# A list planner whose ranks for DVE, ACT and POOL are counted back from TensorE's list, with costs fitted to the trace

## The chip, the cores and the metric

The kernel runs on one core of one Trainium2 chip. The metric is the device time of one execution in microseconds (us), the median of several runs. Engines are named as in the profile: PE is TensorE (its matmuls; PEld its weight loads), DVE is VectorE, ACT is ScalarE, POOL is GpSimd, SP is SyncE.

## The reference

Three stages follow each other over 6016 tokens of width 256, all in float32:

```python
s = kn.transpose(0, 2, 1) @ qn / tau      # 256 x 256 scores of normalised k and q
a = softmax(s)
x = v @ a                                  # 6016 x 256
h = x @ w_in                               # 256 -> 2048
y = (h * sigmoid(1.702 * h)) @ w_out       # 2048 -> 256
gate, val = sigmoid(y @ w_gate), y @ w_val # 256 -> 1536
out = (gate * val) @ w_out2                # 1536 -> 256
```

## The kernel before

The softmax matrix is multiplied into `w_in` first (`m_unit`), so that the first stage is one product of `v` with a 256 x 2048 matrix `m_t`. Each float32 factor is split in two float16 parts, a high part (`gh`, ACT or DVE) and a rest (`gl`, DVE, L314 or L1589), and a product is three matmuls. Tokens come in 12 blocks of 512 (the last has 384). The first two blocks use plain products (`eight`); later ones use Strassen's seven products per 2 x 2 block (`seven`, `gv_pair`, `o_pair`), with additions on DVE and copies on ACT between them. In the first stage a block has 8 units: `h_unit` makes the products into PSUM banks, applies the gelu on ACT (L1181, L1187) and splits the result; `y_unit` multiplies it by `w_out` (L1013 to L1015). In the second stage a block has 6 pairs: `gv_pair` (L1472) with copies (L1480) and sigmoids (L1500) on ACT and adds (L1493), a product (L1524), differences (L1563, L1566, L1569) and splits (L1551, L1589) on DVE, and `o_pair` (L1640). POOL takes some differences and the seven final additions `comb` of each block (L1695). Weights are unpacked (L502, L508, L514), scaled by a power of two and split while the first stage runs: for `w_out` ("o1") that is a chain of small DVE steps ending with `own_wo` (L271), a matmul that spreads it over the partitions (L287), a maximum (L290), two small steps (L299), and the split on ACT and DVE (L311, L314) into `wo`.

All of it is written down first as a list of operations in `Plan`, with engine, cost, and dependencies; `Plan.run` then plays a list schedule with these costs and emits the instructions of each engine in the order found. Each engine runs its own list in order and waits on semaphores. At each step `run` takes the operation that can start first; among those on that engine which can start within a small window (`EPS`, `HOLD`), the one with the lowest rank is preferred. Before, an operation's rank is its place in the program plus a hand-set `delay`:

```python
self.ops.append((fn, engines, deps, i + self.delay, lone))
rank = lambda i: self.ops[i][3]
_, s, e, c, i = min(cand, key=lambda x: (x[1], rank(x[4])))
```

Of the kernel before, what the change touches and what calls it, by code (L numbers as in the profile page):

```python
# [46 lines left out]
class Plan:  # L47
# [53 lines left out]

    def run(self):
        n = len(self.ops)
        after = [[] for _ in range(n)]
# [28 lines left out]
        while ready:  # L133
# [12 lines left out]
            rank = lambda i: self.ops[i][3]  # L146
# [21 lines left out]
def fused_kernel(ctx, tc, q, k, vt, tau, w_in, w_o1, w_g, w_v, w_o2, outt):  # L168
# [180 lines left out]
    def right_ops(z, n, q4, rest, kx, s, ks, after=()):  # L349
# [125 lines left out]
    def w_top(name, i, after=()):  # L475

        wide = w_src[name][1]
        if name in LOOSE:
# [5 lines left out]
            w_op(name, total, ("act", 1.25), r=[("w", name, i)],  # L484
# [10 lines left out]
    def w_f32(name, i, after=()):  # L495
# [30 lines left out]
        w_op(name, mag, ("act", 1.1), r=[kr], w=[kw], after=list(after) + [w_open[name]])  # L526
        w_op(name, shift3, ("dve", 0.68), r=[kw], w=[kw])
        if name in LOOSE:
            w_top(name, i)
        if name in BY_POOL:  # L530
            plan.delay += JOIN * (name == "in")
            w_op(name, sign, ("act", 1.1), r=[kr], w=[kr])
            w_op(name, lambda e: join(0, ALU.logical_shift_right, 29), ("dve", 1.22), r=[kr, kw], w=[kw])
            w_op(name, signed, ("pool", 2.4), r=[kr, kw], w=[kw])
            plan.delay -= JOIN * (name == "in")
        else:
            w_op(name, lambda e: join(1, ALU.bitwise_and, 0x80000000), ("dve", 1.22), r=[kr, kw], w=[kw])
# [42 lines left out]
    def w_split(name, h, lo, i, after=()):  # L580
# [9 lines left out]
        w_op(name, hi, ("act", 1.1), r=r, w=[("wh", name, i)], after=after)  # L590
        w_op(name, low, ("dve", 1.26), r=r + [("wh", name, i)], w=[("wl", name, i)])
# [250 lines left out]
    def softmax(i):  # L842
# [179 lines left out]
    def seven(z, w, left, rl, val):  # L1022
# [8 lines left out]
        def product(a, x, key, start):  # L1031
            def fn(e):
# [8 lines left out]
                op(fn, ("pe", 3 * (w / 2400 + 0.004)), r=rl(a) + [("Th", z, right), ("Tl", z, right)], w=[key])  # L1041
            )

        def copy(dst, key, wk):
            after = a21_users if wk[0] != "rot" and wk not in plan.writer else ()
            op(lambda e: nc.scalar.copy(out=dst, in_=bank(key)[:, :w]), ("act", 0.1 + w / 1150), r=[key], w=[wk],  # L1046
               after=after)

        def add(half, other, ko):
# [729 lines left out]
```

## Time and profile before

| | us |
|---|---|
| median of 3 runs | 1028.23 (1027.2 to 1029.16) |
| the profiled execution's own time | 1027.24 |
| its span, first to last instruction | 1025.2 |
| PE busy | 1016.8 |
| DVE busy | 875.7 |
| ACT busy | 736.6 |
| POOL busy | 122.2 |

In the profile a matmul's end is modelled, so that successive matmuls overlap in the rows; when PE was really held up is read from the distance of two starts, not from a gap. DVE and ACT rows overlap their successor too, by some 0.08 and 0.10 us. A wait is named with what released it.

### The profile page before, as it was taken

The numbers are of one execution on the slowest core, as the hardware profiler recorded it, in microseconds if no ns is written. First come the engines' busy times: TensorE is split into PE (matmuls) and PEld (weight loads), VectorE is DVE, ScalarE is ACT, GpSimd is POOL, SyncE is SP. The second block draws the span as 40 slices with busy tenths as digits, with TensorE's granted clock in tenths as the row PEclk, the third lists the DMA queues.
The fourth block names the chain that finished last, engine by engine and source line by source line (L and its number), as shares of the span: only waits on it lengthen the run. The fifth ranks groups of instructions, "written<-read, shape, count | busy, mean of one in ns | idle before, by whom it ended". The sixth has DMA issues, their size and how long they took to land.

```text
span 1025.2 us, 18922 instructions
## 1 busy us (share of the span) xinstructions
PE 1016.8 (99%) x7709; PEld 767.9 (75%) x7709; DVE 875.7 (85%) x1377; ACT 736.6 (72%) x1193; POOL 122.2 (12%) x145
## 2 busy tenths in 40 slices
PE   9999999999999999999999999999999999999998
PEld 7744456666666666666677788888888888888896
DVE  6999989999888767767598998989889889898984
ACT  6789368877776656556566777787787777787774
POOL 0120100100000000000000002021230330222302
PEclk9999999999999999999999999999999999999999
DMA  9930213210000000000000000000000000000001
GB/s 346 404 121 21 83 42 144 103 62 22 21 1 22 21 1 17 1 1 1 1 2 2 1 22 22 2 21 7 17 22 2 22 21 1 22 7 17 21 3 36
DMA packets 17399, 43.68 MB, mean 43 GB/s; under 512 B 1824, under 2 KB 8224, under 8 KB 15648
## 3 DMA queue, kind: packets, MB, share of 16 engines
q1 hardware_dynamic: 16736, 41.56, 11.3%
q8 instruction: 60, 0.98, 0.4%
q10 hardware_dynamic: 576, 0.92, 0.3%
q14 instruction: 27, 0.22, 0.1%
HBM read 36.31 MB, written 6.16 MB: 41 GB/s over the span
## 4 chain that ended last, share of the span: by engine, by line
PE 91%; DVE 3%; DMA 2%; issue 2%; ACT 1%; POOL 0%; SPq 0%; ACTq 0%; POOLq 0%
PE ps L1472 31%; PE ps L1037 17%; PE ps L1640 13%; PE ps L1015 10%; PE ps L1014 10%; PE ps L1013 10%; PE ps L948 1%; DMA tau<-in_tau 1%; DVE gl L314 1%; DMA m_t<-in_q 1%; DMA m_t<-in_k 1%; DVE vo L314 0%; POOL full_in L524 0%; DVE gf L1051 0%; DVE s_t L314 0%
## 5 line engine op out<-in xcount | busy, mean ns | idle before, releaser
L1472 PE MATMUL ps<-vo,s_t 128*128 128x256 f16 (+1 forms) x3024 | 362.0, 270 | 0.2 <-ACT m_t L1500 0.2
L1472 PEld LDWEIGHTS <-s_t 128*128 128x128 f16 x3024 | 292.6, 98 | 38.2 <-issue 0.6
L1037 PE MATMUL ps<-vo,m_t 128*128 128x256 f16 (+1 forms) x1680 | 217.8, 270 | 0.0
L1037 PEld LDWEIGHTS <-m_t 128*128 128x128 f16 x1680 | 162.6, 98 | 67.9 <-issue 1.0
L1014 PE MATMUL ps<-gl,wo 128*128 128x512 f16 (+1 forms) x348 | 130.2, 374 | 0.0
L1015 PE MATMUL ps<-gh,wo 128*128 128x512 f16 (+1 forms) x348 | 130.2, 374 | 0.0
L1013 PE MATMUL ps<-gh,wo 128*128 128x512 f16 (+1 forms) x348 | 130.2, 374 | 0.0
L1493 DVE TENSOR_TENSOR gf<-ps,m_t 128x512 f32<-128x512 f32 (+1 forms) x144 | 97.3, 676 | 37.2 <-PE ps L1472 31.8
L1500 ACT ACTIVATE m_t<-ps,sgb 128x512 f32<-128x512 f32 (+1 forms) x144 | 97.5, 680 | 41.4 <-PE ps L1472 40.5
L314 DVE SCALAR_TENSOR_TENSOR gl<-gf,sgi,gh 128x1024 f16<-128x1024 f32 (+1 forms) x87 | 109.1, 1255 | 4.2 <-ACT gh L311 3.6
L1046 ACT COPY m_t<-ps 128x256 f32<-128x256 f32 (+1 forms) x160 | 57.5, 364 | 74.4 <-PE ps L1037 73.2
L1480 ACT COPY m_t<-ps 128x512 f32<-128x512 f32 (+1 forms) x144 | 83.0, 576 | 38.7 <-PE ps L1472 34.7
L1051 DVE TENSOR_TENSOR gf<-ps,m_t 128x256 f32<-128x256 f32 (+1 forms) x160 | 65.3, 414 | 42.6 <-ACT m_t L1046 25.6
L1524 DVE SCALAR_TENSOR_TENSOR gf<-gf,m_t 128x1024 f32<-128x1024 f32 (+1 forms) x72 | 88.2, 1229 | 1.9
L1589 DVE TENSOR_TENSOR gl<-ts,gh 128x1024 f16<-128x1024 f32 x60 | 74.4, 1241 | 3.4 <-ACT gh L1586 3.3
L1640 PEld LDWEIGHTS <-wo 128*128 128x128 f16 x720 | 70.3, 98 | 8.0
L1640 PE MATMUL ps<-gh,wo 128*128 128x256 f16 x360 | 76.1, 273 | 0.0
L1695 POOL TENSOR_TENSOR m_t<-m_t 128x256 f32<-128x256 f32 x70 | 65.5, 949 | 67.3 <-ACT m_t L1687 65.1
L1015 PEld LDWEIGHTS <-wo 128*128 128x128 f16 x384 | 37.6, 98 | 43.6
L1204 DVE TENSOR_SCALAR gh<-gf,sgi 128x1024 f16<-128x1024 f32 (+1 forms) x63 | 46.4, 736 | 26.8 <-PE ps L1015 24.6
L1586 ACT CAST gh<-ts 128x1024 f16<-128x1024 f32 x60 | 62.7, 1046 | 6.1 <-DVE ts L1569 3.6
L1181 ACT ACTIVATE gf<-gf,sgs 128x512 f32<-128x512 f32 (+1 forms) x80 | 56.0, 709 | 11.5 <-DVE gf L1051 10.6
(249 smaller groups left out, 1607.1 us busy)
## 6 DMA issues: line engine op xcount, KB each, us to landing
v_raw<-in_vt SPq DMA_DIRECT2D x11, 512.0 KB, 5.0
out_t<-m_t SPq DMA_DIRECT2D x40, 128.0 KB, 1.7
m_t<-in_k SPq DMA_DIRECT2D x9, 512.0 KB, 7.7
m_t<-in_q SPq DMA_DIRECT2D x9, 512.0 KB, 8.6
s_t<-in_w_o SPq DMA_DIRECT2D x3, 1024.0 KB, 4.9
s_t<-in_w_g SPq DMA_DIRECT2D x3, 1024.0 KB, 5.1
s_t<-in_w_v SPq DMA_DIRECT2D x3, 1024.0 KB, 5.0
big<-in_w_in SPq DMA_DIRECT2D x2, 1024.0 KB, 10.5
```

Source lines behind the costliest of these rows:

```text
L314: nc.vector.scalar_tensor_tensor(out=lo, in0=x, scalar=s, in1=h, op0=ALU.mult, op1=ALU.subtract)
L1013: nc.tensor.matmul(ps[:, :n], w_h, x_h, start=first, stop=False)
L1014: nc.tensor.matmul(ps[:, :n], w_h, x_l, start=False, stop=False)
L1015: nc.tensor.matmul(ps[:, :n], w_l, x_h, start=False, stop=last)
L1037: nc.tensor.matmul(dst, l, r, start=start and y == 0, stop=y == 2, skip_group_check=True)
L1472: nc.tensor.matmul(dst, l, r, start=start and f == 0 and y == 0, stop=y == 2, skip_group_check=True)
L1480: op(lambda e: nc.scalar.copy(out=dst, in_=bank(key)[:, : 2 * w]), ("act", 0.12 + 2 * w / 1180), r=[key], w=[wk], after=late_after if wk[0 ...
L1493: nc.vector.tensor_add(quarters(T[kf], half), pairs(bank(kw)), pairs(other))
L1500: nc.scalar.activation(out=quarters(sig_t[ks[1] % 2], half), in_=pairs(bank(key)), func=AF.Sigmoid, scale=T[sk])
L1524: nc.vector.scalar_tensor_tensor(out=v, in0=v, scalar=VSHIFT, in1=sig_t[ks[1] % 2][:, : 4 * w], op0=ALU.mult, op1=ALU.mult)
L1589: nc.vector.tensor_sub(T[name][1][:, : 4 * w], T[kt][:, : 4 * w], T[name][0][:, : 4 * w])
L1640: nc.tensor.matmul(dst, l, r, start=start and p == 0 and y == 0, stop=p == NP2 - 1 and y == 2, skip_group_check=True)
```

## The change

Operations from `plan.first` on (from the first unit of the first stage) get new ranks. The PE operations are laid end to end in the order of their old ranks, which gives each a planned start; from there each DVE, ACT and POOL operation gets a due time, its user's due time less its own cost and 0.17; its rank becomes that of the PE operation planned at that time, and lower still where the due time is negative. The second part is the costs: those of nearly all DVE and ACT operations and of the PE products are set to new values, mostly lower by some per cent. No operation is added or removed; the order in which each engine does them changes, and for operations that two engines can do, the engine.

```diff
+SLACK, EASE = 0.0, 0.0
...
+    def due(self, first):
+
+        ranks = [o[3] for o in self.ops]
+        pe = sorted((i for i in range(first, len(self.ops)) if self.ops[i][1][0][0] == "pe"), key=lambda i: ranks[i])
+        t, at, due = 0.0, [], {}
+        for i in pe:
+            due[i] = t
+            at.append(t)
+            t += self.ops[i][1][0][1]
+        for j in range(len(self.ops) - 1, first - 1, -1):
+            d = due.setdefault(j, t)
+            for i, kind in self.ops[j][2].items():
+                if i >= first and self.ops[i][1][0][0] != "pe":
+                    gap = 0.0 if kind in ("place", "order") else self.LAT + self.ops[i][1][0][1]
+                    due[i] = min(due.get(i, t), d - gap)
+        for i in range(first, len(self.ops)):
+            if self.ops[i][1][0][0] != "pe":
+                x = bisect(at, due[i] + SLACK) - 1
+                ranks[i] = ranks[pe[max(x, 0)]] + min(due[i] + SLACK, 0.0) * 6 + EASE * (due[i] + SLACK - at[max(x, 0)])
+        return ranks
...
-            rank = lambda i: self.ops[i][3]
+            rank = ranks.__getitem__
...
-                op(fn, ("pe", 3 * (w / 2400 + 0.004)), r=rl(a) + [("Th", z, right), ("Tl", z, right)], w=[key])
+                op(fn, ("pe", 3 * (w / 2400 + 0.0023)), r=rl(a) + [("Th", z, right), ("Tl", z, right)], w=[key])
...
-            op(lambda e: nc.scalar.copy(out=dst, in_=bank(key)[:, :w]), ("act", 0.1 + w / 1150), r=[key], w=[wk],
+            op(lambda e: nc.scalar.copy(out=dst, in_=bank(key)[:, :w]), ("act", 0.06 + w / 1200), r=[key], w=[wk],
...
-        op(hi, [("act", 0.14 + 0.93 * f), ("dve", 0.1 + 0.53 * f, GH_DVE)], r=r, w=[k_g],
+        op(hi, [("act", 0.19 + 0.854 * f), ("dve", 0.13 + 0.534 * f, GH_DVE)], r=r, w=[k_g],
```

Over the whole program 25 of the high-part conversions of the first stage (L1204 on DVE, L311 on ACT) move from DVE to ACT and 8 the other way. Of the quarter differences of the second stage (L1566, L1569) 28 move from DVE to POOL and 16 the other way. SP's list is the same but for two neighbouring loads that trade places.

**First place, DVE where the scale of `w_out` is found.** Before, from `own_wo` (the last step ahead of the matmul L287) to the split of `wo`; `mf` and `ms` are sums of `m_t` that the third block's products need, `s_t` and `gl` are rests of units:

```order
L271 TENSOR_SCALAR own_wo_111<-cl_wo_110 128x1
L984 TENSOR_TENSOR mf_858<-m_t 128x1024
L290 TENSOR_REDUCE p_wo_112<-ps 128x1
L989 TENSOR_TENSOR ms_869<-mf_858 128x256
L299 RECIPROCAL s_wo_113<-p_wo_112 128x1
L989 TENSOR_TENSOR ms_869<-mf_858 128x256
L299 TENSOR_SCALAR s_wo_113<-s_wo_113 128x1
L989 TENSOR_TENSOR ms_869<-ms_869,mf_858 128x256
L989 TENSOR_TENSOR ms_869<-mf_858,ms_869 128x256
L314 SCALAR_TENSOR_TENSOR s_t<-y_f,sgi_647,s_t 128x1024
L314 SCALAR_TENSOR_TENSOR wo_87<-big,s_wo_113,wo_87 128x1024 x4
```

And after the change, on the same engine from the same instruction (L295 is now what L271 was, L338 what L314 was):

```order
L295 TENSOR_SCALAR own_wo_111<-cl_wo_110 128x1
L338 SCALAR_TENSOR_TENSOR gl_0_0_690<-gf_0_0_682,sgi_666,gh_0_0_689 128x1024
L314 TENSOR_REDUCE p_wo_112<-ps 128x1
L323 RECIPROCAL s_wo_113<-p_wo_112 128x1
L323 TENSOR_SCALAR s_wo_113<-s_wo_113 128x1
L323 RECIPROCAL s_v_117<-p_v_116 128x1
L338 SCALAR_TENSOR_TENSOR gl_0_1_730<-gf_0_1_720,sgi_666,gh_0_1_729 128x1024
L338 SCALAR_TENSOR_TENSOR wo_87<-big,s_wo_113,wo_87 128x1024 x4
```

The two rests `gl` of the first units, which stood far ahead of `own_wo` before, now stand behind it, and the sums have gone behind the split. In PE's list the matmul L287 on `own_wo` stands 7 products (of `eight`) earlier than before, and the first product of `y_unit` (L1013 on `gh`) follows it after 3 products, where there were 4.

**Second place, ACT in the eighth block of the first stage.** `gf_7_3` is the gelu of unit 3 (in two halves), COPY is a bank that PE will write again; before:

```order
L311 ACTIVATE vo<-tt,s_v_201 128x1024
L1245 COPY big<-ps 128x512 x2
L1181 ACTIVATE gf_7_3_3491<-ps,sgs_3194 128x512
L1046 COPY ps<-ps 128x256 x2
L1046 COPY m_t<-ps 128x256 x2
L1181 ACTIVATE gf_7_3_3491<-gf_7_3_3491,sgs_3194 128x512
```

And after the change, around the same gelu:

```order
L1205 ACTIVATE gf_7_3_3466<-ps,sgs_3025 128x512
L335 ACTIVATE gh_7_1_3479<-gf_7_1_3363,sgi_3026 128x1024
L1205 ACTIVATE gf_7_3_3466<-gf_7_3_3466,sgs_3025 128x512
L335 ACTIVATE vo<-tt,s_v_201 128x1024
L1269 COPY big<-ps 128x512
L1070 COPY ps<-ps 128x256
L1269 COPY big<-ps 128x512
L1070 COPY ps<-ps 128x256
L1070 COPY m_t<-ps 128x256 x3
```

A conversion `gh_7_1` that DVE did before now stands here between the two gelu halves, and the copies of the next units come behind the long operations in one row.

**Third place, DVE at the end of the ninth block of the second stage.** `gf_8_5` belongs to that block's last pair, `gf_9_0` to the next block's first; each pair has two adds from PSUM, and the second frees the bank that the next pair's product L1472 writes. Before, from one second add to the next:

```order
L1493 TENSOR_TENSOR gf_8_5_9823<-ps,m_t 128x2x256
L1524 SCALAR_TENSOR_TENSOR gf_8_5_9823<-gf_8_5_9823,m_t 128x1024
L1493 TENSOR_TENSOR gf_9_0_9882<-ps,m_t 128x2x256
L1589 TENSOR_TENSOR gl_8_4_9874<-ts_8_4_9832,gh_8_4_9873 128x1024
L1563 TENSOR_TENSOR ts_8_5_9906<-gf_8_5_9823 128x512
L1551 TENSOR_TENSOR m_t<-gf_8_5_9823,m_t 128x768
L1566 TENSOR_TENSOR ts_8_5_9906<-gf_8_5_9823,ts_8_5_9906 128x256
L1493 TENSOR_TENSOR gf_9_0_9882<-ps,m_t 128x2x256
```

And after the change, up to the same add of `gf_9_0` (the last row; the second add of `gf_8_5` stands two rows ahead of the first row shown, with one split `vo` of 128x768, L338, between):

```order
L1549 SCALAR_TENSOR_TENSOR gf_8_5_9772<-gf_8_5_9772,m_t 128x1024
L1576 TENSOR_TENSOR m_t<-gf_8_4_9685,m_t 128x768
L1614 TENSOR_TENSOR gl_8_4_9798<-ts_8_4_9748,gh_8_4_9797 128x1024
L1588 TENSOR_TENSOR ts_8_5_9848<-gf_8_5_9772 128x512
L338 SCALAR_TENSOR_TENSOR vo<-tt,s_y_235,vo 128x1024
L1518 TENSOR_TENSOR gf_9_0_9871<-ps,m_t 128x2x256
L1479 TENSOR_TENSOR sgb_9884<-qb_234,kg 128x1
L1594 TENSOR_TENSOR ts_8_5_9848<-gf_8_5_9772,ts_8_5_9848 128x256
L384 TENSOR_TENSOR tt<-big 128x384
L387 TENSOR_TENSOR tt<-big,tt 128x192
L1576 TENSOR_TENSOR m_t<-gf_8_5_9772,m_t 128x768
L1518 TENSOR_TENSOR gf_9_0_9871<-ps,m_t 128x2x256
```

The preparation of a later block's input (`tt`, `vo`, L338, L384, L387), which stood elsewhere before, has come in between. From the second add of `gf_8_4` to the second add of `gf_9_0` DVE's list has 15 instructions before and 24 after the change; PE's list has, between the product that the first of these adds reads and the one that writes the bank again after the second, 35 products (16 of `gv_pair`, of 6 matmuls each, and 19 of `o_pair`, of 3) after the change.

## Rows read from the trace of the kernel before

**Rows 1.** The page, busy time by engine, and granted PE clock in 40 slices.

```profile
PE 1016.8 (99%) x7709; PEld 767.9 (75%) x7709; DVE 875.7 (85%) x1377; ACT 736.6 (72%) x1193; POOL 122.2 (12%) x145
...
PEclk9999999999999999999999999999999999999999
```

**Rows 2.** Busy time by stretch: PE, PEld, DVE, ACT, POOL, clock, DMA, GB/s.

```profile
75.00:150.00 75.00, 75.00 (x372) 36.17 (x371) 68.72 (x104) 48.63 (x57) 3.57 (x3) 1.00 0.15 50
150.00:325.00 175.00, 174.96 (x1174) 114.73 (x1173) 162.93 (x295) 133.72 (x248) 7.97 (x12) 1.00 0.15 53
325.00:525.00 200.00, 200.00 (x1405) 134.62 (x1404) 139.40 (x261) 121.97 (x245) 6.09 (x9) 1.00 0.03 8
...
600.00:1000.00 400.00, 399.99 (x3701) 359.59 (x3700) 363.39 (x488) 307.05 (x466) 83.47 (x97) 1.00 0.04 13
```

**Rows 3.** PE's own waits: us in total, times, longest.

```profile
PE ps L877 <- ACT ex L857: 1.3, 2, 1.0
...
PE ps L1472 <- ACT m_t L1500: 0.2, 1, 0.2
```

**Rows 4.** PE in order of time where a start came late: start, length, instruction.

```profile
254.94 0.38 PE L1015 MATMUL ps<-gh,wo 128*128 128x512 f16 x1
255.32 0.49 PE L1037 MATMUL ps<-vo,m_t 128*128 128x256 f16 x3
...
531.88 0.82 PE L1472 MATMUL ps<-vo,s_t 128*128 128x256 f16 x6
532.93 0.82 PE L1472 MATMUL ps<-vo,s_t 128*128 128x256 f16 x6 [0.24 <-ACT m_t L1500]
...
962.82 0.27 PE L1640 MATMUL ps<-gh,wo 128*128 128x256 f16 x1
963.10 1.14 PE L1472 MATMUL ps<-vo,s_t 128*128 128x256 f16 x9
```

**Rows 5.** ACT in order of time, the table load at 531.

```profile
530.90 1.28 ACT L1500 ACT_TABLE_LOAD   x1
```

**Rows 6.** PE in order of time, the start of the first stage.

```profile
82.25 0.38 PE L1013 MATMUL ps<-vo,m_t 128*128 128x512 f16 x1
...
91.31 0.22 PE L287 MATMUL ps<-ident_b,own_wo 128*128 128x128 bf16 x1
...
96.55 0.38 PE L1013 MATMUL ps<-gh,wo 128*128 128x512 f16 x1
```

**Rows 7.** DVE in order of time, the same stretch.

```profile
68.68 0.75 DVE L1204 TENSOR_SCALAR gh<-gf,sgi 128x1024 f16<-128x1024 f32 x1
...
69.80 0.75 DVE L314 SCALAR_TENSOR_TENSOR m_t<-ps,rss,m_t 128x512 f16<-128x512 f32 x1 [0.36 <-ACT m_t L311]
...
80.81 1.29 DVE L314 SCALAR_TENSOR_TENSOR vo<-v_raw,s_v,vo 128x1024 f16<-128x1024 f32 x1 [0.32 <-ACT vo L311]
...
89.51 0.15 DVE L271 TENSOR_SCALAR own_wo<-cl_wo 128x1 uint32<-128x1 uint32 x1
...
91.57 0.29 DVE L290 TENSOR_REDUCE p_wo<-ps 128x1 f32<-128x128 f32 x1 [0.78 <-PE ps L287]
...
94.88 1.28 DVE L314 SCALAR_TENSOR_TENSOR wo<-big,s_wo,wo 128x1024 f16<-128x1024 f32 x1 [0.24 <-ACT wo L311]
```

**Rows 8.** ACT in order of time, the same stretch.

```profile
93.72 4.25 ACT L311 ACTIVATE wo<-big,s_wo 128x1024 f16<-128x1024 f32 x4
```

**Rows 9.** Groups by line and shape: busy, mean ns of one | idle before.

```profile
L311 ACT ACTIVATE gh<-gf,sgi 128x1024 f16<-128x1024 f32 x23 | 26.4, 1148 | 5.2 <-PE ps L1015 5.0
```

**Rows 10.** DVE in order of time, from `gf_8_4` to `gf_9_0`.

```profile
898.37 0.69 DVE L1493 TENSOR_TENSOR gf<-ps,m_t 128x512 f32<-128x512 f32 x1
...
908.78 0.68 DVE L1493 TENSOR_TENSOR gf<-ps,m_t 128x512 f32<-128x512 f32 x1
```

**Rows 11.** POOL and DVE in order of time, where both run.

```profile
919.35 7.98 POOL L1695 TENSOR_TENSOR m_t<-m_t 128x256 f32<-128x256 f32 x7 [3.73 <-ACT m_t L1687]
...
921.97 1.75 DVE L314 SCALAR_TENSOR_TENSOR vo<-tt,s_y,vo 128x1024 f16<-128x1024 f32 x1
```

More of the change, by code (lines that the diff above doesn't have):

```diff
@@ L1 @@
+from bisect import bisect
 from contextlib import ExitStack
@@ L100, in op @@
         return i
+    def due(self, first):
[17 more added lines that the diff above has]
+        return ranks
     def run(self):
         n = len(self.ops)
+        ranks = self.due(self.first)
         after = [[] for _ in range(n)]
@@ L377, in right_ops @@
         for fn, m in ((t13, 2), (t2, 1), (t4, 1)):
-            op(fn, ("dve", 0.12 + m * w / 930), r=kx, w=[k], after=after)
+            op(fn, ("dve", 0.08 + m * w / 960), r=kx, w=[k], after=after)
         split(3, 4, lambda: tt[:, : 4 * w], [k])
@@ L482, in total @@
                 )
[L484 removed]
+            w_op(name, total, ("act", 1.05), r=[("w", name, i)],
                  w=[("ws", name, i)], after=after)
@@ L524, in signed @@
             nc.gpsimd.tensor_mul(x, x, half(name, i, 1).bitcast(F32))
-        w_op(name, mag, ("act", 1.1), r=[kr], w=[kw], after=list(after) + [w_open[name]])
-        w_op(name, shift3, ("dve", 0.68), r=[kw], w=[kw])
+        w_op(name, mag, ("act", 1.0), r=[kr], w=[kw], after=list(after) + [w_open[name]])
+        w_op(name, shift3, ("dve", 0.61), r=[kw], w=[kw])
         if name in LOOSE:
@@ L589, in w_split @@
         r = [("w", name, i), ("wsc", name)]
-        w_op(name, hi, ("act", 1.1), r=r, w=[("wh", name, i)], after=after)
-        w_op(name, low, ("dve", 1.26), r=r + [("wh", name, i)], w=[("wl", name, i)])
+        w_op(name, hi, ("act", 1.0), r=r, w=[("wh", name, i)], after=after)
+        w_op(name, low, ("dve", 1.2), r=r + [("wh", name, i)], w=[("wl", name, i)])
     def s_ratio(after=()):
@@ L1001, in m_sums @@
         for n_, (out, x, y, how) in enumerate(chain):
-            op(lambda e, out=out, x=x, y=y, how=how: sums(e, out, x, y, how), ("dve", 0.4),
+            op(lambda e, out=out, x=x, y=y, how=how: sums(e, out, x, y, how), ("dve", 0.35),
                r=[kf] + ([ks] if n_ else []), w=[ks] if n_ == 0 else [("ms", fg)])
@@ L1347, in fused_kernel @@
     m_units(M_FIRST)
+    plan.first = len(plan.ops)
     steps = [(b, u) for b in range(NBLK) for u in range(NU)]
@@ L1422, in o2_sums @@
         r = [(k, "o2", i) for k in ("wh", "wl") for i in range(ch * 4 * w // PW, -(-(ch + 1) * 4 * w // PW))]
-        op(blocks4, ("dve", 1.2), r=r, w=[kf], after=after)
+        op(blocks4, ("dve", 1.14), r=r, w=[kf], after=after)
         add, sub = nc.vector.tensor_add, nc.vector.tensor_sub
@@ L1439, in dst @@
             return so[:, y, :, 2 * ch : 2 * ch + 2, :]
-        op(lambda e: nc.scalar.copy(out=dst(0), in_=src()), ("act", 1.1), r=[ks, ("os", ch)], w=[("soh", ch)], after=after)
+        op(lambda e: nc.scalar.copy(out=dst(0), in_=src()), ("act", 1.0), r=[ks, ("os", ch)], w=[("soh", ch)], after=after)
         op(lambda e: nc.vector.tensor_sub(dst(1), src(), dst(0)), ("dve", 1.2), r=[ks, ("os", ch), ("soh", ch)],
@@ L1475, in product @@
             i = 2 * p * P // NB
-            first_op.append(op(fn, ("pe", 6 * (w / 2400 + 0.004)),
+            first_op.append(op(fn, ("pe", 6 * (w / 2400 + 0.0023)),
                                r=[("Sh", i, a), ("Sl", i, a), ("Th", z, right), ("Tl", z, right)], w=[key]))
         def copy(dst, key, wk):
-            op(lambda e: nc.scalar.copy(out=dst, in_=bank(key)[:, : 2 * w]), ("act", 0.12 + 2 * w / 1180), r=[key], w=[wk],
+            op(lambda e: nc.scalar.copy(out=dst, in_=bank(key)[:, : 2 * w]), ("act", 0.06 + w / 600), r=[key], w=[wk],
                after=late_after if wk[0] != "rot" else ())
```

62 lines of the change are left out of this document (31 added, 31 removed).

## The prediction

> **What bounds the kernel now.** The page comes first: PE is busy 1016.8 of 1025.2 us, the granted clock is full in all 40 slices, and DVE (875.7) and ACT (736.6) have slack [rows 1]. The reader is to see that a change which leaves PE's work alone can win only what PE loses by waiting. [...] From 600 to 1000 us 3701 matmuls take 400.0 us, 0.108 us each, so a matmul there follows the one before without pause.
>
> The chain of waits names few for PE [rows 3]: 1.3 us on L857's exponentials are in the softmax ahead of the first unit, where DMA and the scores set the pace, and only one is behind 75 us. Because a PE row's end is modelled, I look instead at the distance of starts. After 60 us only eight starts are more than 0.04 us late, 1.24 us together. Three of them stand in the rows [rows 4]: L1037 at 255.32 comes 0.38 after a matmul of 512 columns, for which 0.21 is the rule in that list (0.17 late); at 963.10 a matmul comes 0.28 after one that needs 0.11 (0.17); and the largest, 0.41, ends at 532.93. In front of this last one ACT loads a table, 1.28 us from 530.90 [rows 5], because the gelu gives way to the sigmoid. Both lists hold the same table loads, so I leave that wait where it is. The other seven make 0.83 us. That is what better ranks can win back in the body of the program, and it is less than a tenth of a per cent.
>
> What lies ahead of 60 us is bound by loads and by the softmax, and the last products and stores of the final block keep their order; the lists first differ on ACT at about 45 us, on DVE at about 62 and on PE at 82.
>
> **The change part by part.** PE does the same products with the same number of columns. The new ranks and the new costs answer one question together, the order, so they are priced together; none costs or saves engine time by itself except by the engine that takes an operation. 17 net conversions go from DVE to ACT: 1.15 us each there [rows 9] for 0.75 on DVE [rows 7], so ACT gains about 19.6 us of work and DVE loses 12.8; 12 net differences leave DVE for POOL. From 150 to 525 us ACT is busy 255.7 of 375 us [rows 2], so both fit on average. The question is only whether a PE operand comes later than its turn at a place where nothing is in reserve.
>
> *Waits of before.* Seven waits, 0.83 us. A new order moves all neighbours, so these can go altogether; I take −0.8, with bounds 0 and −1.2 (the last if the table wait goes too).
>
> *The scale of `w_out`.* This is the place where PE's own order moves. L287 stands 7 products earlier. A product is three matmuls of 512 columns whose starts are 0.43 us apart here, 1.295 us for the three, so PE comes to L287 at 91.31 − 9.06 = 82.25 us and to the first product of `y_unit` at 82.25 + 3 × 1.295 + 0.05, about 86.2 [rows 6]. DVE must have `own_wo` by then. Before, it takes 20.83 us from L1204 at 68.68 to `own_wo` at 89.51 [rows 7]. In the new order there drop out of this stretch four rests `gl` or `s_t` and one split `vo` (rows of this shape are 1.28 long, 1.20 from start to start), one `gh` (0.67 a step), about 0.45 of small steps, and the two idles of 0.36 and 0.32 behind ACT [rows 7]: 6.0 + 0.67 + 0.45 + 0.68 = 7.8. That leaves 13.0; I add 0.5 because ACT does an unpacking ahead of a high part that DVE waits for. So `own_wo` is ready at about 68.68 + 13.5 = 82.2, just as PE arrives. From there the chain goes on: a `gl` (1.20) now stands ahead of the maximum L290 (0.29 [rows 7]), then two small steps of 0.19, the high part on ACT (1.06 a step [rows 8], about 1.13 to its end), the rest on DVE (1.28 [rows 7]): 4.3 us. Against 3.9 on PE's side, the product waits about 0.3 us. What is late next: eight products queued behind it on PE, and a gelu behind the four conversions of `wo` (4.25 us together [rows 8]), about 0.2. Term +0.5; bounds 0.2 and 1.2, the last if `own_wo` is 0.7 us later than worked out.
>
> *Copies behind conversions on ACT.* In the second place ACT now has a conversion between the two halves of a gelu, and a row of copies behind. The adds on DVE that need these copies free PE's banks. Before, with 33 conversions on ACT, six of the seven waits lie between 150 and 525 us and come to 0.65 us, 0.02 for each conversion; without the one at 313 us, behind a maximum of `v` (0.20), it is 0.014. At these prices 50 conversions cost between 0.7 and 1.0 us; I take +0.8, since costs near the true step leave an operation no more reserve than before. It would stand mostly where DVE's adds near 363, 402 and 441 us free a bank. Bounds: 0, because PE may have other work in its queue at each place, and 2.0, 0.04 for each of the 50.
>
> *The end of the ninth block of the second stage.* From second add to second add DVE takes 908.78 − 898.37 = 10.41 us for 15 instructions, 0.69 a step [rows 10]. 24 instructions at that step are 16.7 us. PE has 35 products in between, 16 × 6 + 19 × 3 = 153 matmuls, 16.5 us at 0.108. The margin is gone: any delay there is one of PE's. Term +0.3, bounds 0 (the small rows among the 24 are shorter than the mean) and 0.9 (two collisions with POOL, next).
>
> *Differences on POOL.* While POOL runs its seven additions from 919.35, a rest on DVE takes 1.75 us [rows 11] where the same shape takes 1.28 elsewhere [rows 7], 0.47 more. For 12 more POOL operations that is up to 12 × 0.47 = 5.6 us of DVE, against its 36.6 us idle between 600 and 1000 us [rows 2]; its price for PE is nil except where a margin is nil, and that is in the range of the term before. [...]
>
> **Sum.** −0.8 + 0.5 + 0.8 + 0.3 = +0.8 us. The profiled execution took 1027.24, so 1028.0 on its scale. The runs' median is 1028.23, 1.0 above that execution, so the forecast is **1029.0 us**: a little more PE waiting, in other places than before. A difference of 0.2%, 2.06 us, is about what a measurement of this kernel can tell from none.
>
> **The rivals.** *The waits go.* The ranks are counted back from PE's own list, and if each operand comes in time all of 0.8 to 1.2 us go: 1027.0 to 1027.4 against the median. For it speaks that the average load leaves room on every engine; against it that a rank only prefers among operations that could start nearly at once, and that DVE keeps 90% busy from 600 to 1000 us. The case that the new order changes nothing visible (1028.2) belongs here too.
>
> *`own_wo` late (slower).* If DVE does one maximum of `v` (1.2) and one `gl` (1.2) more ahead of `own_wo` than I count, L287 stands at the head of PE's queue for 2.4 us and everything behind it with it: 1029.0 + 2.4 = 1031.4. It decides for "slower" from 1.3 us of lateness on. For it: the margin is nil by my sum. Against: an item in the list is counted, not guessed; only waits on ACT and loads could shift it.
>
> *DVE blocked by POOL (slower).* Eight collisions more at places without margin, 8 × 0.47 = 3.8, give 1032.8; from four on it is slower by the bound. For it: the cost per collision is in the rows. Against: there are few places without margin, and DVE idles behind PE in most of the second stage.
>
> **How the numbers follow.** The likeliest case, waits that change places, has 0.73, mostly 1028.0 to 1030.2; the waits that go, or nothing visible, 0.10; `own_wo` late 0.08; DVE blocked 0.06; a gain above the 1.2 us that the trace has on offer, from the softmax or the end, 0.03. The range 1026.9 to 1031.5 leaves out the top of the last rivals and the gain beyond 1.3 us. A gain over 0.2% is 0.03; slower than 0.2%, above 1030.3, takes the two slow rivals and a few hundredths of the first case, 0.17; within, 0.80.
>
> **What would show it.** Right: in the rows of PE's start distances a late start of a few tenths at L287 or at the first L1013 on `gh` near 86 us; late L1037 behind DVE adds between 300 and 525 us; a late L1472 near 910 us; those at 255, 271 and 313 us gone; the one behind the table load still there; L1204's count on DVE down by 17, the differences L1566 and L1569 on POOL up by 12, PE's count unchanged. Wrong: PE late by over 1 us at L287, or DVE's rests of 1.75 us beside POOL in many places with late L1472 behind them; or no late start after 60 us at all, by which the ranks would have done what my margins deny.

## The result and the profile after

The changed kernel takes 1036.59 us (median of 5, 1035.98 to 1037.01) against 1027.2 us of the kernel before beside it: ratio 1.0086, 95% interval 1.0071 to 1.0101. It is slower, by more than the forecast range allowed. The profiled execution is one of 1036.59 us with a span of 1034.5, 9.3 us more than before.

First the page and the windows by stretch of the changed kernel, to be read beside [rows 1] and [rows 2] (columns as there):

```profile
PE 1022.1 (99%) x7709; PEld 769.5 (74%) x7709; DVE 872.9 (84%) x1348; ACT 752.9 (73%) x1210; POOL 149.9 (14%) x157
```

```profile
525.00:575.00 50.00, 50.00 (x394) 38.31 (x393) 43.37 (x66) 36.08 (x54) 0.00 (x0) 1.00 0.01 1
575.00:596.00 21.00, 20.46 (x152) 14.66 (x150) 18.67 (x30) 14.85 (x23) 3.01 (x3) 1.00 0.01 5
596.00:604.00 8.00, 4.77 (x42) 4.10 (x42) 4.43 (x8) 2.32 (x5) 0.71 (x1) 1.00 0.15 57
604.00:608.00 4.00, 3.40 (x17) 2.34 (x17) 2.19 (x4) 1.14 (x4) 0.00 (x0) 0.58 0.00 0
608.00:625.00 17.00, 17.00 (x157) 15.24 (x156) 15.06 (x20) 13.97 (x20) 2.96 (x2) 1.00 0.01 1
```

Most of what was lost, 6.35 of 9.0 us, lies in one place, 595 to 608 us: PE idles 3.2 us of eight, and in the four behind it the granted clock is 0.58. PE's own waits, as in [rows 3], name two that were not there before:

```profile
PE ps L1497 <- ACT m_t L1505: 3.4, 1, 3.4
...
PE ps L1497 <- DVE gf L1518: 1.0, 1, 1.0
```

And PE in order of time, as in [rows 4]:

```profile
600.92 0.27 PE L1665 MATMUL ps<-gh,wo 128*128 128x256 f16 x1
604.60 1.44 PE L1497 MATMUL ps<-vo,s_t 128*128 128x256 f16 x6 [3.40 <-ACT m_t L1505]
605.83 0.42 PE L1665 MATMUL ps<-gh,wo 128*128 128x256 f16 x1
```

Six matmuls from 604.60 to 605.83 are about 0.21 us each, where 0.108 is usual, and the granted clock is 0.50 from 604.60 to 607.00 us; 15 starts in a row are like that. So the late starts of this place come to 1.13 (at 596.42) + 3.57 (at 604.60) + 1.65 (the 15 at half clock and the one ahead of them) = 6.35 us. All starts more than 0.04 us late behind 60 us make 10.26, before 1.24; the difference, 9.0, is the span's 9.3 but for some tenths in the prologue. The other 3.9 us are 32 late starts of 0.05 to 0.41 us.

The chain of waits blames ACT's copy L1505 and DVE's add, but both had been done in time if their own engines had not waited. Going back from them in the changed kernel, one engine after the other, first ACT and DVE, then POOL in order of time:

```profile
602.44 1.04 ACT L1611 CAST gh<-ts 128x1024 f16<-128x1024 f32 x1 [3.88 <-POOL ts L1594]
...
603.97 0.58 ACT L1505 COPY m_t<-ps 128x512 f32<-128x512 f32 x1
```

```profile
589.23 0.15 DVE L295 TENSOR_SCALAR own_y<-cl_y 128x1 uint32<-128x1 uint32 x1
...
594.55 0.16 DVE L323 RECIPROCAL s_y<-p_y 128x1 f32<-128x1 f32 x1 [1.96 <-POOL p_y L302]
...
597.01 0.43 DVE L1591 TENSOR_TENSOR ts<-gf,ts 128x256 f32<-128x256 f32 x1
```

```profile
581.15 1.31 POOL L1591 TENSOR_TENSOR ts<-gf,ts 128x256 f32<-128x256 f32 x1 [64.13 <-DVE ts L1588]
586.87 1.32 POOL L1594 TENSOR_TENSOR ts<-gf,ts 128x256 f32<-128x256 f32 x1 [4.40 <-DVE ts L1591]
594.14 0.38 POOL L302 PARTITION_ALL_REDUCE p_y<-own_y  x1 [5.96 <-issue]
601.69 0.71 POOL L1594 TENSOR_TENSOR ts<-gf,ts 128x256 f32<-128x256 f32 x1 [7.17 <-issue]
```

The reader is to see two idles of POOL that nothing in the profile ends ("issue"). The all-reduce of `p_y` (the maximum of the last block of `y` over the partitions) has its input at 589.38 and starts at 594.14; the difference behind it has its input at 597.44 and starts at 601.69. DVE stands 1.96 us behind the first, ACT 3.88 us behind the second, each with its other work queued up, and PE behind both. In the kernel before the same all-reduce ran 40.7 us earlier, and 28.6 us ahead of the first difference:

```profile
553.46 0.35 POOL L278 PARTITION_ALL_REDUCE p_y<-own_y  x1 [37.37 <-DVE own_y L271]
582.45 0.73 POOL L1569 TENSOR_TENSOR ts<-gf,ts 128x256 f32<-128x256 f32 x1 [28.64 <-DVE ts L1566]
```

POOL's list says what is between. Of the kernel before, from the last all-reduce but one, and of the changed one, from the same place (a row with ISA and no operand stands wherever the kind of operation changes; in the built program it is an instruction to reload a library, `PseudoReloadLibraryIndex`, index 1 ahead of all-reduces and 0 ahead of differences; it has no row in the profile):

```
L278 ISA p2_y0_233<-own_y0_232 128x1
L278 ISA p2_y1_238<-own_y1_237 128x1
L1569 ISA
L1569 TENSOR_TENSOR ts2_1_0_5847<-gf2_1_0_5779,ts2_1_0_5847 128x256
```

```
L302 ISA p2_y0_233<-own_y0_232 128x1
L1591 ISA
L1591 TENSOR_TENSOR ts2_1_0_5828<-gf2_1_0_5757,ts2_1_0_5828 128x256
L1594 TENSOR_TENSOR ts2_1_1_5877<-gf2_1_1_5823,ts2_1_1_5877 128x256
L302 ISA
L302 ISA p2_y1_238<-own_y1_237 128x1
L1594 ISA
L1594 TENSOR_TENSOR ts2_1_2_5989<-gf2_1_2_5906,ts2_1_2_5989 128x256
```

Behind its unpacking of weights, POOL's list of before goes over once to the all-reduces (ahead of 73.38 us) and once from them to the differences, both at leisure; the changed one then goes back and over again.

### The profile page after: what moved, and what is told of

The parts are those of the page before. It is cut to its first block, busy times and chain, and to the rows that moved or that the text cites. A ratio compares the mean times of both kernels' runs of the same rounds, so it can differ in the third digit from the quotient of the medians.

```text
span 1034.5 us, 18983 instructions
## 1 busy us (share of the span) xinstructions
PE 1022.1 (99%) x7709; PEld 769.5 (74%) x7709; DVE 872.9 (84%) x1348; ACT 752.9 (73%) x1210; POOL 149.9 (14%) x157
## 4 chain that ended last, share of the span: by engine, by line
PE 90%; issue 3%; DVE 3%; DMA 2%; ACT 2%; POOL 0%; SPq 0%; DVEq 0%; POOLq 0%; ACTq 0%
PE ps L1497 31%; PE ps L1061 17%; PE ps L1665 13%; PE ps L1037 9%; PE ps L1039 9%; PE ps L1038 9%; PE ps L972 1%; DMA big<-in_w_in 1%; DVE big L538 1%; DMA m_t<-in_q 1%; ACT wo L335 0%; DMA m_t<-in_k 0%; ACT sq L748 0%; ACT junk L504 0%; POOL full_in L548 0%
## 5 line engine op out<-in xcount | busy, mean ns | idle before, releaser
L1497 PE MATMUL ps<-vo,s_t 128*128 128x256 f16 (+1 forms) x3024 | 370.4, 271 | 4.5 <-ACT m_t L1505 3.4
L1061 PE MATMUL ps<-vo,m_t 128*128 128x256 f16 (+1 forms) x1680 | 222.3, 270 | 0.0
L1518 DVE TENSOR_TENSOR gf<-ps,m_t 128x512 f32<-128x512 f32 (+1 forms) x144 | 97.4, 677 | 28.6 <-PE ps L1497 16.3
L338 DVE SCALAR_TENSOR_TENSOR gl<-gf,sgi,gh 128x1024 f16<-128x1024 f32 (+1 forms) x87 | 109.0, 1253 | 3.0 <-ACT gh L335 2.7
L1505 ACT COPY m_t<-ps 128x512 f32<-128x512 f32 (+1 forms) x144 | 83.1, 577 | 35.5 <-PE ps L1497 34.1
L1549 DVE SCALAR_TENSOR_TENSOR gf<-gf,m_t 128x1024 f32<-128x1024 f32 (+1 forms) x72 | 92.5, 1285 | 3.4
L1720 POOL TENSOR_TENSOR m_t<-m_t 128x256 f32<-128x256 f32 x70 | 70.2, 1014 | 119.2 <-ACT m_t L1712 117.4
L1614 DVE TENSOR_TENSOR gl<-ts,gh 128x1024 f16<-128x1024 f32 x60 | 75.3, 1255 | 7.7 <-ACT gh L1611 7.4
L1665 PE MATMUL ps<-gh,wo 128*128 128x256 f16 x360 | 79.1, 273 | 0.0
L1205 ACT ACTIVATE gf<-ps,sgs 128x512 f32<-128x512 f32 (+1 forms) x80 | 53.9, 674 | 20.2 <-PE ps L1061 19.7
L1576 DVE TENSOR_TENSOR m_t<-gf,m_t 128x768 f16<-128x768 f32 x60 | 60.0, 1000 | 4.1 <-ACT m_t L1573 3.9
```

Source lines behind the costliest of these rows:

```text
L338: nc.vector.scalar_tensor_tensor(out=lo, in0=x, scalar=s, in1=h, op0=ALU.mult, op1=ALU.subtract)
L1061: nc.tensor.matmul(dst, l, r, start=start and y == 0, stop=y == 2, skip_group_check=True)
L1497: nc.tensor.matmul(dst, l, r, start=start and f == 0 and y == 0, stop=y == 2, skip_group_check=True)
L1505: op(lambda e: nc.scalar.copy(out=dst, in_=bank(key)[:, : 2 * w]), ("act", 0.06 + w / 600), r=[key], w=[wk], after=late_after if wk[0] != ...
L1518: nc.vector.tensor_add(quarters(T[kf], half), pairs(bank(kw)), pairs(other))
L1549: nc.vector.scalar_tensor_tensor(out=v, in0=v, scalar=VSHIFT, in1=sig_t[ks[1] % 2][:, : 4 * w], op0=ALU.mult, op1=ALU.mult)
```

## The experiments

Theory K: POOL pays some 6 to 7 us whenever it goes from differences to an all-reduce or back, and here twice while somebody waits. Its rival, theory M: the new order has no reserve anywhere, and the stall at 600 us is only the largest of its late starts. The table sums all starts of PE that come over 0.04 us late, in us by stretch, in the profiled execution of each run; the ratio is to the kernel before on the same chip.

| run | median | ratio (95%) | 60–100 | 100–525 | 525–580 | 580–625 | 625–960 | 960– | sum |
|---|---|---|---|---|---|---|---|---|---|
| before | | | 0 | 0.66 | 0.41 | 0 | 0 | 0.17 | 1.24 |
| changed | 1036.59 | 1.0086 (1.0071–1.0101) | 0.41 | 1.49 | 0.32 | 6.35 | 0.89 | 0.80 | 10.26 |
| extra_exposed | 1037.63 | 1.0092 (1.0078–1.0106) | 0 | 0.64 | 0.40 | 9.18 | 0 | 0.18 | 10.40 |
| extra_hidden | 1027.74 | 0.9999 (0.9990–1.0008) | 0 | 0.64 | 0.40 | 0 | 0 | 0.18 | 1.21 |
| no_switch | 1035.97 | 1.0077 (1.0065–1.0090) | 0.40 | 1.56 | 0.32 | 4.90 | 0.90 | 0.80 | 8.88 |
| no_switch3 | 1030.41 | 1.0030 (1.0020–1.0041) | 0.35 | 1.34 | 0.33 | 0.19 | 0.90 | 0.80 | 3.91 |
| early_y | 1030.97 | 1.0030 (1.0019–1.0041) | 0.38 | 1.44 | 0.09 | 0 | 1.47 | 0.79 | 4.17 |
| ranks_only | 1037.14 | 1.0083 (1.0069–1.0096) | 0.73 | 0.45 | 0.08 | 3.76 | 4.15 | 0.07 | 9.23 |
| costs_only | 1031.82 | 1.0038 (1.0026–1.0051) | 1.25 | 1.58 | 0.42 | 0 | 1.13 | 0.63 | 5.01 |
| early_y_gh | 1030.47 | 1.0023 (1.0013–1.0033) | 0.74 | 0.87 | 0.31 | 0 | 1.09 | 0.97 | 3.98 |
| early_y_t | 1030.28 | 1.0028 (1.0017–1.0040) | 0.38 | 1.34 | 0.09 | 0 | 1.49 | 0.66 | 3.96 |
| early_y_copies | 1032.60 | 1.0046 (1.0033–1.0059) | 0.42 | 1.18 | 0 | 0 | 3.64 | 0 | 5.24 |
| early_y_lat | 1029.41 | 1.0017 (1.0008–1.0026) | 1.96 | 1.25 | 0 | 0 | 0 | 0 | 3.21 |
| first_stage | 1029.18 | 1.0013 (1.0004–1.0022) | 0.18 | 0.70 | 0 | 0 | 1.38 | 0 | 2.25 |
| mix_1 | 1027.26 | 0.9995 (0.9986–1.0004) | 0.18 | 0.37 | 0 | 0 | 0 | 0 | 0.55 |
| mix_2 | 1026.60 | 0.9991 (0.9983–1.0000) | 0 | 0.06 | 0 | 0 | 0 | 0 | 0.06 |
| mix_3 | 1026.03 | 0.9989 (0.9981–0.9998) | 0 | 0.06 | 0 | 0 | 0 | 0 | 0.06 |

The kernel before took 1027.55 to 1027.73 us beside the experiments (medians of 15 to 27 executions).

**One all-reduce added to the kernel before.** It is put behind the last difference of a pair, and a library reload comes with it on either side; no other instruction of any engine moves. Pair `2_1_2` is at 595 us, pair `2_1_4` at 608.

```diff
         def t4(e):
             eng(e).tensor_sub(s(3), q(3), s(2))
+            if name == "2_1_2":                  # extra_hidden: "2_1_4"
+                nc.gpsimd.partition_all_reduce(vec("dum"), first["i_in"], P, bass_isa.ReduceOp.max)
```

> The kernel before, with one all-reduce on a constant, which nobody reads, put on POOL behind the difference at 595.4 us; nothing else moves on any engine. Theory K: 6 us to go over, 7 us to come back, so the next difference comes at about 609.6 instead of 600.1, ACT's conversion behind it at 610 instead of 602.5, and PE loses 5 to 8 us: 1032 to 1036 us. Theory M: POOL is idle most of the time and one operation of 0.4 us costs nothing, 1027 to 1028 us.

> The same extra all-reduce, behind the difference at 607.8 us, where POOL is idle until 623.6. Theory K: over and back by about 622, in time, no change: 1027 to 1028.5 us. If the extra instruction hurts in another way than by a late difference, as late as in its sister run.

POOL of extra_exposed in order of time, and of extra_hidden:

```profile
595.36 0.73 POOL L1569 TENSOR_TENSOR ts<-gf,ts 128x256 f32<-128x256 f32 x1 [12.22 <-ACT m_t L1500]
602.04 0.38 POOL L1571 PARTITION_ALL_REDUCE dum<-i_in  x1 [5.95 <-ACT m_t L1500]
609.14 0.71 POOL L1569 TENSOR_TENSOR ts<-gf,ts 128x256 f32<-128x256 f32 x1 [6.73 <-issue]
```

```profile
610.93 0.73 POOL L1569 TENSOR_TENSOR ts<-gf,ts 128x256 f32<-128x256 f32 x1 [7.01 <-DVE ts L1566]
617.57 0.38 POOL L1571 PARTITION_ALL_REDUCE dum<-i_in  x1 [5.91 <-issue]
626.72 0.73 POOL L1569 TENSOR_TENSOR ts<-gf,ts 128x256 f32<-128x256 f32 x1 [8.78 <-DVE ts L1566]
```

In both the all-reduce of a constant, whose input was there all along, starts 5.95 and 5.91 us after the difference. In the first the next difference waits 6.73 us more for nothing shown, and PE with it (7.23 us late, and 1.95 at half clock, 0.57 granted from 612 to 616 us, which the expectation left out: 9.2 instead of 5 to 8, so that the time is above the 1032 to 1036 expected). In the second the 8.78 us behind the all-reduce are ended by DVE: the way back was over before the operand came, and the time is that of before. One instruction costs 10 us or nothing, by where it stands. K is shown; M cannot say it.

**The changed kernel with the first differences on DVE.** no_switch keeps pairs 0 and 1 of the block on DVE, no_switch3 pairs 0 to 2.

```diff
         def either(m):
+            if name in ("2_1_0", "2_1_1"):       # no_switch3: and "2_1_2"
+                return ("dve", 0.08 + m * w / 960)
             return [("dve", 0.08 + m * w / 960)] * ("dve" in T_BY) + ...
```

> The changed kernel, but the quarter differences of the first two pairs of the second stage's first Strassen block stay on DVE, so that all of POOL's all-reduces stand ahead of its first difference again; some ten DVE rows around them shift. Theory K (POOL pays about 6 us each time it goes from differences to the all-reduce and back): POOL's idle of 5.96 and 7.17 us by issue at 588 to 602 us goes, and with it 6.4 us of PE (1.1 + 3.6 of late starts and 1.6 of half clock): about 1030.2 us. Theory M (thin margins of the new order everywhere, the stall at 601 us being only the largest): the other late starts add up as before and a stall of some us comes again near 600: 1034 us or more.

> As the run that kept two pairs on DVE, with the third pair's differences on DVE too: there POOL did one difference right behind the late all-reduce at 593.4 us, and it came 6.75 us later. POOL's next difference is then that at about 612. Theory K: the stall at 600 us and its half clock go, 6.3 us against the changed kernel, about 1030.2 us, with some 4 us of small late starts left. Theory M: a stall of some us comes back near 600 behind another engine, 1034 us or more.

POOL of no_switch, and of no_switch3:

```profile
593.40 0.35 POOL L302 PARTITION_ALL_REDUCE p_y<-own_y  x1 [76.17 <-DVE own_y L295]
600.49 0.71 POOL L1594 TENSOR_TENSOR ts<-gf,ts 128x256 f32<-128x256 f32 x1 [6.75 <-issue]
```

```profile
593.45 0.35 POOL L302 PARTITION_ALL_REDUCE p_y<-own_y  x1 [76.17 <-DVE own_y L295]
607.53 0.97 POOL L1591 TENSOR_TENSOR ts<-gf,ts 128x256 f32<-128x256 f32 x1 [13.73 <-ACT m_t L1505]
```

The first run missed its number, 1036.0 in place of 1030.2, and M's was nearer. But the rows say why: the all-reduce, which now follows another all-reduce, starts 0.17 us behind DVE's `own_y`, so that it is the change of kind and not the all-reduce by itself that costs 6 us; only the way back to the third pair's difference is still too late, 6.75 us behind it. One change of kind of the two was gone, and 3.31 us of late start with 1.4 us of half clock behind it remained. With that difference on DVE too the second way falls into an idle of 13.73 us that ACT ends, and 6.2 us are back: 1030.41, where K said 1030.2.

**The last maximum of `y` by its old rank.** POOL keeps its differences.

```diff
+        for i in self.keep:                      # the operations of y_max(NBLK - 1)
+            ranks[i] = self.ops[i][3]
         return ranks
```

> The changed kernel, but the maximum and the scale's exponent of the last block of y keep the rank of before, so their all-reduce stands ahead of POOL's first difference; POOL keeps its differences. Theory K: about 1030.2 us, as the run before, one code change on POOL, behind 517 us and unseen. If the late all-reduce costs by something other than the two changes (DVE's list around it), 1034 us or more.

The all-reduce is back at 554.67 us, ahead of the first difference at 580.32, and no start between 580 and 625 us is late. Time 1030.97, near the 1030.2 expected. So two different cures give back the same 5.6 to 6.2 us, and 0.3% remains in both.

**Ranks alone and costs alone.** ranks_only has the old costs with `due`, costs_only the new costs with `ranks = [o[3] for o in self.ops]`.

> The old costs with the new ranks. POOL's list goes over to differences and back to the all-reduce once more, as in the changed kernel. Theory K: a stall of 4 to 7 us near 590 to 605 us, 1032 to 1036 us. Theory M, if the thin margins come from the smaller costs: under 1030 us.

> The new costs with the old ranks. POOL's list has one change of code, as before. Theory K: no stall over 1 us, 1027 to 1030 us. Theory M (costs without reserve make the late starts): 1030 us or more, with many late starts of 0.05 to 1 us.

The ranks bring the changes of kind (POOL's list of ranks_only goes over twice more, that of costs_only does not). Their stall is 3.76 us in three late starts, a little under K's 4 to 7: 0.89 at 601.24 and 1.46 at 608.92, behind waits of DVE for POOL of 2.43 and 1.85 us, and 1.41 at 613.93 behind a DVE row of 2.02 us beside a long POOL row. The costs alone bring late starts nearly everywhere, 1031.82: that is M's case (1030 or more) and not K's (1027 to 1030). So K explains the stall, and M has a share in the rest. The ranks alone have fewer late starts than before from 100 to 525 us, 0.45 against 0.66, but 4.15 us of them from 625 to 960 us, which neither theory named and which put the time above K's 1036. There the planner, with DVE's long costs, gives whole half differences (L1588, 128x512) to POOL. PE, DVE and POOL of ranks_only at one of these places:

```profile
712.15 0.60 PE L1497 MATMUL ps<-vo,s_t 128*128 128x256 f16 x4 [0.77 <-DVE gf L1518]
```

```profile
708.34 2.03 DVE L1576 TENSOR_TENSOR m_t<-gf,m_t 128x768 f16<-128x768 f32 x1
```

```profile
707.30 2.24 POOL L1588 TENSOR_TENSOR ts<-gf 128x512 f32<-128x512 f32 x1 [1.65 <-DVE gf L1549]
```

DVE's L1576 takes 0.95 us elsewhere and 2.03 beside POOL's 2.24: 1.08 us more, and PE's start behind the next add is 0.93 late.

**What makes the other 0.3%.** Three theories: R, the plan keeps too little reserve at each step; O, the order by due time itself makes operands late; P, POOL's additional differences slow DVE. Four runs on early_y. early_y_gh puts each high-part conversion on the engine of before, early_y_t each quarter difference. early_y_copies plans ACT's copies at their old costs, and early_y_lat plans every handover between engines longer:

```diff
-    LAT = 0.17
+    LAT = 0.3                                   # early_y_lat
-("act", 0.06 + w / 1200), r=[key], w=[wk],      # early_y_copies, and L1505 likewise
+("act", 0.1 + w / 1150), r=[key], w=[wk],
```

> As the run with the early maximum of y, and each high-part conversion of the first stage on the engine that did it before. If the late L1061 behind ACT copies between 150 and 525 us come from conversions that went to ACT, 0.8 to 1.2 us less than that run, about 1029.2 us; if they come from ranks that leave no reserve, the same as that run.

> The same run with each quarter difference on the engine that did it before (36 on POOL). Theory P (POOL's additional work slows DVE where both read SBUF): the 1.5 us of late starts between 625 and 960 us go, about 1029.5 us. Theories R and O: the same as that run within 0.5 us, 1030.5 to 1031.5 us.

> The run with the early maximum of y (1031.0), with ACT's copies out of PSUM planned at the old, longer costs. In that run 4.2 us of late starts are left behind 60 us, some 2.9 of them behind ACT copies. Theory R (the new costs leave a copy no reserve): most of the 2.9 us go, about 1028.3 us. Theory O (the order by due time is what makes them late): no change, 1030.5 to 1031.5 us.

> The same run with the planned handover from engine to engine at 0.30 us in place of 0.17, for the schedule and the due times alike; the costs stay new. Theory R: reserve by another way, late starts of 0.05 to 0.2 us go, 2.5 to 4 us less, 1027 to 1028.5 us. Theory O: 1030.5 us or more.

Conversions: from 100 to 525 us the late starts go from 1.44 to 0.87, but others come at the start, and the time falls by 0.5, inside both intervals. Differences: no change where theory P wanted it, 1.47 and 1.49 between 625 and 960 us. But the run is no clean test of P: with the 36 quarter differences fixed, the planner put six half differences (128x512) on POOL, and all its differences took 51.1 us there, against 54.0 in early_y and 26.2 before; the late starts stand at other places. P is neither shown nor excluded. Copies: theory R in this form falls. The small late starts behind copies went in the second stage, but four of 0.89 us came there instead; at 645 us, for one, three DVE rows in a row are 0.5 us longer beside POOL's final additions. The longer handover: from 200 us on early_y has 28 late starts, 3.5 us; here one of 0.06 is left. The time, 1029.41, lies between the two forecasts, for three new late starts of about 1 us stand ahead: at 63 us on POOL's `full_in`, at 89 on DVE's `wo`, and one at 188 us, whose rows on PE and ACT are

```profile
188.72 0.49 PE L1064 MATMUL ps<-vo,m_t 128*128 128x256 f16 x3 [0.89 <-ACT m_t L1073]
```

```profile
187.28 1.12 ACT L529 ACTIVATE big<-s_t 128x1024 f32<-128x1024 f32 x1 [1.38 <-DMA s_t<-in_w_g]
188.31 0.63 ACT L1073 COPY m_t<-ps 128x256 f32<-128x256 f32 x2
```

ACT stands 1.38 us behind a weight load, with a copy queued behind it that PE needs.

**Due-time ranks where they are good.** first_stage has the old costs, and the new ranks from the second block of the first stage to its end. mix_1 to mix_3 have the new ranks, the new costs, `LAT = 0.3` and the early maximum, from the second, third and fourth block on; ahead of that, ranks, costs and handover of before.

```diff
     for x, step in enumerate(steps):
+        if x == 3 * NU:                          # mix_3
+            plan.first = len(plan.ops)
```

> The old costs; due-time ranks only from the second block of the first stage to its end, all else by the old ranks, the last maximum of y early by itself, one change of code on POOL. In the run of ranks alone this stretch had 0.5 us of late starts where before has 1.1. If the new ranks are good where costs keep their reserve: 0.4 to 0.9 us of late starts behind 60 us, 1026.7 to 1027.5 us, not to be told from before. Theory O: 1029 us or more.

> Old ranks, old costs and the old handover up to the second block of the first stage; from there the due-time ranks, the new costs, a handover of 0.30 us, and the early maximum of y. Theory R (due-time order is sound where the plan keeps reserve): no late start over 0.1 us behind about 100 us but that behind the table load, if that; under 0.5 us in all, 1026.6 to 1027.3 us. If the two late starts of 0.85 and 1.05 us near 90 and 190 us in the run with the longer handover come from the due-time order or the handover after the start, one of them is back here.

> The same from the third block on. Theory R: under 0.5 us of late starts, 1026.6 to 1027.3 us. A late start of 1 us near 190 us is back if it belongs to the third and later blocks.

> The same from the fourth block on, all up to it as before. Theory R: under 0.5 us of late starts, 1026.6 to 1027.3 us. No late start before 200 us, as in the kernel before.

first_stage missed, and its 1029.18 is O's number; but its late starts are not where the new ranks are. The first stage is as before, and the second, with old ranks behind another state, has one of 1.0 (at 719.95) and one of 0.33 us, both behind DVE rows of 1.75 us beside POOL's final additions. The mixes did what R says, mix_1 not quite: it has 0.55 us where under 0.5 was expected, two late starts of 0.15 and 0.16 between 185 and 192 us among them. The windows of mix_3, to be read beside [rows 2]:

```profile
75.00:525.00 450.00, 450.00 (x2956) 286.43 (x2955) 365.29 (x650) 315.10 (x562) 13.77 (x24) 1.00 0.10 32
525.00:600.00 75.00, 75.00 (x596) 58.05 (x595) 65.03 (x97) 54.85 (x82) 3.81 (x3) 1.00 0.02 8
600.00:1000.00 400.00, 400.00 (x3707) 359.89 (x3705) 369.49 (x479) 307.19 (x466) 120.66 (x106) 1.00 0.04 13
```

PE is busy in every hundredth of 925 us; one start is 0.06 late. The late starts at 90 and 190 us belonged to the start of the program. mix_3 is 1026.03 us, 0.9989 of before, an interval that only just leaves out 1; 1.18 us fewer late starts are 0.11% as well. Which of ranks, costs and handover is needed for it was not taken apart.

## Why the prediction was wrong

The step that failed is **differences on POOL** in the change part by part. It priced POOL's 12 more operations by what they do to DVE, 0.47 us for a collision, "nil except where a margin is nil", and took no notice of the order on POOL, though another kind of operation stood in that list. The due-time ranks count the all-reduce of the last `y` back from its user, so it is planned as late as its 0.5 us of cost allow, behind the first differences. The plan has no price for a change of kind; measured it is 5.95 us one way (extra_exposed) and 7.17 the other (the changed kernel). The trace of before did not show it at any price: its two changes of kind lay in 8.9 and 28.6 us of POOL's idle time, each ended by DVE, and both the rows and the list were read for PE, DVE and ACT. Nor was it among the rivals, all of which looked for the loss on the engines that PE waits for by name.

Of the other steps:

- *Bound and ceiling.* Right: PE's work is the same, and all that was lost or won is late starts and the clock behind the longest of them. mix_3 won back the 1.2 us that the prediction named as the most there is, the one behind the table load with them; that this one must stay was wrong (in the changed kernel PE still has products of the last block to do at 532.70, when the table is loaded).
- *Waits of before*, −0.8: they went, all 1.24.
- *The scale of `w_out`*, +0.5 (0.2 to 1.2): the steps came as worked out, and 0.41 was lost, not at the product on `wo` but behind it. (A product there is six matmuls 0.216 us apart, not three 0.43 apart; the 1.295 us for it is right.) In the changed kernel, DVE, PE and ACT in order of time:

```profile
82.29 0.14 DVE L295 TENSOR_SCALAR own_wo<-cl_wo 128x1 uint32<-128x1 uint32 x1
```

```profile
82.62 0.22 PE L311 MATMUL ps<-ident_b,own_wo 128*128 128x128 bf16 x1
...
88.94 0.38 PE L1039 MATMUL ps<-gh,wo 128*128 128x512 f16 x1
89.56 0.38 PE L1037 MATMUL ps<-vo,m_t 128*128 128x512 f16 x1 [0.24 <-ACT y_f L1211]
```

```profile
84.24 4.27 ACT L335 ACTIVATE wo<-big,s_wo 128x1024 f16<-128x1024 f32 x4 [0.42 <-DVE s_wo L323]
88.42 2.09 ACT L1211 ACTIVATE y_f<-ps,sgs 128x1024 f32<-128x1024 f32 x2
```

  `own_wo` is ready at 82.4 (82.2 forecast). What is late is the gelu `y_f` (L1211) behind the four conversions of `wo`, as named, 0.41 in place of about 0.2.
- *Copies behind conversions*, +0.8 (0 to 2.0): 1.49 us of late starts from 100 to 525 us, nearly all right behind ACT's copies and not, as said, behind the DVE adds that need them. The term was mis-sized, by half. By early_y_gh the engine of the conversions has 0.6 of it. The prediction took an operation's reserve to be no more than before; that a smaller reserve made the rest fits early_y_lat, where the small ones went, and is not shown by itself.
- *Ninth block*, +0.3 (0 to 0.9): nothing was lost there. From second add to second add DVE took 914.70 − 898.96 = 15.7 us for the 24 instructions, 1.0 less than the 16.7 worked out, and no start of PE between 898.11 and 939.89 us is late. The tightest place by that count was not one. Behind 525 us the changed kernel has, without the stall, 17 other late starts, 2.0 us in all, behind DVE adds or ACT copies; no term named them.

```profile
898.96 0.69 DVE L1518 TENSOR_TENSOR gf<-ps,m_t 128x512 f32<-128x512 f32 x1 [0.31 <-PE ps L1497]
...
914.70 0.68 DVE L1518 TENSOR_TENSOR gf<-ps,m_t 128x512 f32<-128x512 f32 x1
```

- *DVE blocked by POOL* as a rival: real, but 0.75 us here and not 3.8. Four late starts of 0.18 to 0.20 us (773.81, 856.93, 898.11 and 939.89) stand behind adds that follow two DVE rows of 1.5 to 1.75 us beside POOL's final additions, where 1.22 is usual. One of them, DVE and POOL:

```profile
894.04 1.75 DVE L1549 SCALAR_TENSOR_TENSOR gf<-gf,m_t 128x1024 f32<-128x1024 f32 x1
895.71 1.74 DVE L1614 TENSOR_TENSOR gl<-ts,gh 128x1024 f16<-128x1024 f32 x1
897.38 0.68 DVE L1518 TENSOR_TENSOR gf<-ps,m_t 128x512 f32<-128x512 f32 x1
```

```profile
891.68 6.36 POOL L1720 TENSOR_TENSOR m_t<-m_t 128x256 f32<-128x256 f32 x5
```

  Where margins are smaller still (ranks_only, early_y_copies) it is dearer than the 0.47 of the row: up to 1.08.

Without POOL's changes of kind the late starts add up to −1.24 + 0.41 + 1.49 + 2.0 = +2.7 us instead of +0.8: right in direction, 1030.4 to 1031.0 in the two kernels without them, and in the range, but 2.0 of it at places that no term named.

## What to carry to other kernels

When a change reorders lists, read every engine's list for changes of kind, on POOL above all, and not only for the order of what the bound engine waits for: a cost that a trace hides in idle time is not in any row, and comes out when the idle time is used. A planner that puts work as late as its costs allow needs these costs whole (what a change of kind costs included) and a reserve at each handover. Here fitted costs without it lost 0.3%, and the same costs and ranks with 0.13 us more per handover, behind the first blocks, lost nothing.

## What the hardware showed that was not expected

- POOL took 5.91 to 6.01 us to go from subtractions to an all-reduce (extra_hidden 5.91, extra_exposed 5.95, the changed kernel 5.96, ranks_only 6.01) and 6.7 to 7.2 us to go back (extra_exposed 6.73, no_switch 6.75, the changed kernel 7.17), with a library reload in the program at each change. Both begin when the operation before ends, whether or not the next one's operand is there (in the changed kernel the operands came 1.2 and 2.9 us later), so they cost nothing in an idle stretch (13.7 us in no_switch3).
- Behind the late starts of 3.57 us (the changed kernel, 604.60) and 7.23 us (extra_exposed, 611.47) PE's next matmuls took about 0.21 us for 256 columns where 0.108 is usual, in the changed kernel at a granted clock of 0.50 from 604.60 to 607.00 us, which cost 1.65 and 1.95 us more. Behind late starts of 0.89 us (ranks_only, 601.24) and 1.13 us (the changed kernel, 596.42) the next ones kept their 0.108.
- In ranks_only a DVE row with two SBUF inputs (L1576) took 1.08 us more beside a long POOL row (0.95 to 2.03); POOL's row ran on for 1.20 us of it (to 709.54). POOL's rows are longer too: in the changed kernel its differences of 128x256 take 1.31 to 1.70 us where they start while such a DVE row runs (L338, L1576 or L1614), and 0.71 to 0.74 alone or from a start beside DVE's adds from PSUM (L1518).
